# Moving the Q and K row transposes from TensorE to VectorE in a segment-recurrent attention kernel

## Chip, cores, metric

One core of one Trainium2 chip. The metric is device time in microseconds (us), median of several executions. The kernel before takes 2215.26 us (2214.29 to 2218.69, 4 runs).

## The reference, cut

```python
# A: 64 segments of 32 tokens, one after the other; B is a gated FFN over all tokens, done before the loop
for s in range(n_seg):                                   # S=2048, seg_len=32, M=8, Dm=640, H=32, Dh=192
    h = concat([mem, x[:, 32*s:32*s+32]], axis=1)        # 40 rows
    q, k, v = (einsum('btd,dhe->bhte', h, W) for W in (Wq, Wk, Wv))
    p = softmax(where(mask, einsum('bhqe,bhke->bhqk', q, k) * scale, -1e9))
    o = einsum('bhte,hed->btd', einsum('bhqk,bhke->bhqe', p, v), Wo)
    mem = o[:, :M]                                       # the next segment needs this
    outs.append(o[:, M:])
return g * concat(outs) + (1 - g) * ffn                  # g = sigmoid(x . gate_w)
```

The recurrence through `mem` makes the 64 segments serial. Every segment reads all of Wq, Wk, Wv and Wo, 31 MB; the kernel keeps part of that in SBUF and fetches the rest anew in every segment.

## The kernel before, where the change touches it

After about 292 us of preparation (the FFN, and the part of Q and K that does not depend on `mem`) comes the loop of 64 segments. The 32 heads go in four octets of 8 heads (1536 columns). Weights are cut into 84 pieces of a segment; 60 stay resident in SBUF and 24 are streamed in every segment through a ring of five slots, issued in program order from the SP queue when a slot comes free. A cost table (`COST`) places the 24 streamed pieces evenly over the estimated time of a segment.

Q (and K) of an octet is computed with the 32 tokens as the stationary operand. Four column tiles of TensorE work at once, each on 384 columns, so the result is four strips of rows [32 tokens, 384]. Scores need the transpose of that, so the rows are copied to SBUF, transposed by TensorE, and copied back once more:

```python
def cmode(s, m, o, bank):                                # m: 0 = Q, 1 = K
    for k in range(KT):                                  # KT = 5
        g_, rg_ = piece(s, (m, o, k))
        S_.add("pe", [lambda e, ...: e.matmul(ps[32*j:32*j+32, bank, 0:384], Hb[hb][:, k, 0:L],
            g_[:, 384*j:384*(j+1)], ..., tile_position=(0, 32*j)) for j in range(4)], ...)
def rows_evac(bank):                                     # ScalarE: ps -> rows_sb (one buffer)
    ...
def row_transp(s, m, o):                                 # three 128x128 TensorE transposes
    bank = misc_bank(); pv = psb(bank)
    S_.add("pe", [lambda e, c=c: e.transpose(pv[:, c*128:(c+1)*128], rows_sb[:, c*128:(c+1)*128], ident)
                  for c in range(3)], ...)
    # Q: one VectorE copy to Qs; K: three ScalarE copies to Ks     [cut]
PROG = [("q",0), ("k",0), ("tq",0), ("v",0), ("tk",0),   # order of the stages of one segment
        ("q",1), ("k",1), ("sc",0), ("tq",1), ("v",1), ("tk",1),
        ("q",2), ("k",2), ("pt",0), ("sc",1), ("tq",2), ("pv",0), ("v",2), ("tk",2), ...]   # [cut]
```

`sc` is scores and the whole softmax, `pt` the transpose of the probabilities with its evacuation, `pv` P times V, `wo` the output projection. Every fourth segment also computes a second V for the leftover tokens.

## Time and profile before

| | before |
|---|---|
| time | 2215.26 us |
| mean of 62 segments (between memory evacuations) | 29.55 us; every fourth 30.92 |
| of that: Q/K/V phase, Wo phase | 19.45, 10.10 us |
| DMA in the loop | 9.26 MB per segment, 313 GB/s, share 0.93 |

The two phases are my cut at the first Wo matmul of each segment, with the windows view over each part.

The page of the kernel before: busy times of the whole execution, and of its costliest groups those that the change touches (engine, operation, output<-input, count, busy us, mean ns of one, then idle time ahead of them and who ended it). PE is TensorE's matmuls, PEld its weight loads, DVE is VectorE, ACT is ScalarE, POOL is GpSimd.

```profile
PE 1912.3 (86%) x41834; PEld 1231.3 (55%) x41862; DVE 943.6 (42%) x3184; ACT 799.7 (36%) x2248; POOL 273.6 (12%) x1210
...
L871 PE MATMUL ps<-arena 128*32 128x384 bf16 x10240 | 488.1, 330 | 69.6 <-DMA arena<-in_A_Wk_dram 23.6
...
L883 PE MATMUL ps<-arena 128*128 128x128 bf16 x1536 | 175.9, 223 | 32.0 <-ACT arena L877 31.9
...
L894 ACT ACTIVATE arena<-ps 64x128 bf16<-64x128 bf16 x512 | 136.8, 267 | 6.3
L887 DVE COPY arena<-ps 128x384 bf16<-128x384 bf16 x256 | 89.4, 349 | 102.0 <-PE ps L883 102.0
```

L871 are the Q and K matmuls, L883 the row transposes (1536 of them, 176 us of busy PE), L894 and L887 two of the copies behind them. The 176 us are tempting, but PE is not simply the limit, as the windows view over the loop shows (us, then busy time of each engine in the order above, granted clock, DMA share, GB/s; the granted clock is the share of its full clock that TensorE was given):

```profile
353.48:2185.74 1832.26, 1585.06 (x39121) 1065.21 (x39121) 835.57 (x2957) 701.85 (x2062) 258.51 (x1146) 0.99 0.93 313
```

The DMA engines are occupied for 93% of the loop while PE is for 87%. The list of waits of PE inside the loop (353 to 2186 us; who waited for whom, us in total, times, longest):

```profile
PE ps L991 <- DVE arena L977: 38.2, 109, 0.4
PE ps L1020 <- DVE arena L1007: 36.4, 105, 0.5
PE ps L905 <- DMA arena<-in_A_Wv_dram: 27.7, 40, 1.8
PE ps L1020 <- DMA arena<-in_A_Wo_dram: 23.2, 43, 2.0
PE ps L905 <- ACT arena L877: 21.4, 40, 0.8
PE ps L871 <- DMA arena<-in_A_Wk_dram: 20.6, 40, 1.2
...
PE ps L871 <- DMA arena<-in_A_Wq_dram: 13.0, 26, 1.1
PE ps L883 <- ACT arena L877: 12.0, 41, 0.3
```

84 us are waits for weight pieces, 83 us for VectorE, 56 us for ScalarE. The timeline of PE (start, duration, then as above) shows what one group of row transposes costs in place:

```profile
1041.29 0.34 PE L883 MATMUL ps<-arena 128*128 128x128 bf16 x3
1041.56 1.81 PE L905 MATMUL ps<-arena 128*32 128x384 bf16 x40
1043.30 0.34 PE L883 MATMUL ps<-arena 128*128 128x128 bf16 x3
1043.57 1.88 PE L871 MATMUL ps<-arena 128*32 128x384 bf16 x40
```

From the start of a group to the next start is 0.27 us, and there are eight groups per segment.

### The profile page before, as it was taken

What the parts mean: (1) busy time and instruction counts of PE and PEld (TensorE: products, weight loads), DVE (VectorE), ACT (ScalarE), POOL (GpSimd) and SP (SyncE); (2) the same over time, 40 slices, a digit from 0 to 9 for tenths busy, and PEclk for the clock granted to TensorE, in tenths of its full rate; (3) what the DMA queues carried; (4) which work ended last, traced back from release to release, by engine and by line L of the source; (5) the groups of instructions that cost most, each with busy time, mean ns of one, the idle gap of its engine ahead of it and who ended that gap; (6) DMA issues with size and microseconds to landing.
All of it is one profiled execution on the core that took longest, in us unless ns stands there. A gap on an engine that the chain in (4) does not pass through costs nothing.

```text
span 2220.5 us, 94985 instructions
## 1 busy us (share of the span) xinstructions
PE 1912.3 (86%) x41834; PEld 1231.3 (55%) x41862; DVE 943.6 (42%) x3184; ACT 799.7 (36%) x2248; POOL 273.6 (12%) x1210
## 2 busy tenths in 40 slices
PE   7999958888888888888888888888888888888887
PEld 3544425555555555555565655555555655555655
DVE  2222223444444444444444444444444544444444
ACT  2222223334333333343333333333333334333333
POOL 0000001111111111111111111111111111111111
PEclk9999989999999999999999999999999999999999
DMA  9203579999999999999999999999999999999998
GB/s 370 88 13 112 150 236 331 322 303 316 301 318 307 324 303 311 305 316 312 319 320 311 316 300 320 306 313 310 320 302 321 309 322 311 315 315 316 310 309 278
DMA packets 363257, 642.75 MB, mean 289 GB/s; under 512 B 60498, under 2 KB 231770, under 8 KB 362842
## 3 DMA queue, kind: packets, MB, share of 16 engines
q1 hardware_dynamic: 311770, 601.01, 80.2%
q10 hardware_dynamic: 51072, 35.66, 5.4%
q8 instruction: 327, 5.36, 0.9%
q14 instruction: 88, 0.72, 0.1%
HBM read 618.74 MB, written 17.83 MB: 287 GB/s over the span
## 4 chain that ended last, share of the span: by engine, by line
PE 46%; DMA 32%; DVE 14%; ACT 3%; issue 3%; ACTq 2%; SPq 0%; DVEq 0%
PE ps L871 12%; DMA arena<-in_A_Wv_dram 10%; DMA arena<-in_A_Wo_dram 9%; PE ps L1020 9%; DMA arena<-in_A_Wk_dram 8%; PE ps L905 7%; DMA arena<-in_A_Wq_dram 4%; DVE arena L974 4%; PE ps L804 3%; PE ps L883 2%; PE ps L742 2%; PE ps L739 2%; ACTq L819 2%; PE ps L757 2%; DVE ps L954 2%
## 5 line engine op out<-in xcount | busy, mean ns | idle before, releaser
L871 PE MATMUL ps<-arena 128*32 128x384 bf16 x10240 | 488.1, 330 | 69.6 <-DMA arena<-in_A_Wk_dram 23.6
L1020 PE MATMUL ps<-arena 128*128 128x40 bf16 x15360 | 457.9, 180 | 64.8 <-DVE arena L1007 38.1
L1020 PEld LDWEIGHTS ps<-arena 128*128 128x128 bf16 x15360 | 428.9, 96 | 88.8 <-DVE arena L1007 49.5
L871 PEld LDWEIGHTS ps<-arena 128*32 128x32 bf16 x10240 | 247.1, 97 | 254.6 <-DMA arena<-in_A_Wk_dram 63.2
L905 PE MATMUL ps<-arena 128*32 128x384 bf16 x6400 | 324.4, 331 | 53.3 <-DMA arena<-in_A_Wv_dram 30.2
L877 ACT ACTIVATE arena<-ps 128x384 bf16<-128x384 f32 x512 | 249.8, 488 | 181.0 <-PE ps L871 105.1
L974 DVE TENSOR_TENSOR arena<-ps,arena 128x320 bf16<-128x320 bf16 x256 | 125.8, 491 | 387.0 <-PE ps L972 387.0
L835 POOL COPY arena<-arena 128x96 bf16<-128x96 bf16 x256 | 67.4, 263 | 1665.0 <-PE ps L937 1138.3
L956 ACT ACTIVATE ps<-ps 104x160 f32<-104x160 f32 x256 | 71.9, 281 | 494.5 <-DVE ps L954 494.5
L905 PEld LDWEIGHTS ps<-arena 128*32 128x32 bf16 x6400 | 144.6, 96 | 175.5 <-DMA arena<-in_A_Wv_dram 59.2
L883 PE MATMUL ps<-arena 128*128 128x128 bf16 x1536 | 175.9, 223 | 32.0 <-ACT arena L877 31.9
L1001 ACT ACTIVATE arena<-ps 128x320 bf16<-128x320 f32 x256 | 112.3, 439 | 215.4 <-PE ps L993 213.8
L991 PE MATMUL ps<-arena 128*128 128x160 bf16 (+1 forms) x768 | 130.5, 260 | 57.1 <-DVE arena L977 39.6
L916 ACT ACTIVATE arena<-ps 128x384 bf16<-128x384 f32 x256 | 125.6, 491 | 139.0 <-PE ps L905 138.7
L839 POOL COPY arena<-arena 64x32 bf16<-64x32 bf16 (+1 forms) x768 | 165.4, 215 | 47.3
L883 PEld LDWEIGHTS ps<-arena 128*128 128x128 bf16 x1536 | 88.1, 98 | 135.7 <-ACT arena L877 91.1
L952 DVE TENSOR_REDUCE arena<-ps 104x4 f32<-104x160 f32 x256 | 80.9, 316 | 149.3 <-PE ps L937 149.3
L894 ACT ACTIVATE arena<-ps 64x128 bf16<-64x128 bf16 x512 | 136.8, 267 | 6.3
L887 DVE COPY arena<-ps 128x384 bf16<-128x384 bf16 x256 | 89.4, 349 | 102.0 <-PE ps L883 102.0
L993 PE MATMUL ps<-arena 128*128 128x64 bf16 (+1 forms) x768 | 124.5, 202 | 4.0 <-ACT arena L877 4.0
L958 DVE TENSOR_REDUCE arena<-ps 104x4 f32<-104x160 f32 x256 | 83.1, 325 | 99.8 <-ACT ps L956 99.8
L991 PEld LDWEIGHTS ps<-arena 128*128 128x128 bf16 x768 | 72.3, 97 | 91.2 <-DVE arena L977 90.7
(81 smaller groups left out, 1886.3 us busy)
## 6 DMA issues: line engine op xcount, KB each, us to landing
arena<-in_A_Wo_dram SPq DMA_DIRECT2D x591, 320.0 KB, 4.7
arena<-in_A_Wv_dram SPq DMA_DIRECT2D x398, 384.0 KB, 5.2
arena<-in_A_Wk_dram SPq DMA_DIRECT2D x340, 384.0 KB, 5.3
arena<-in_A_Wq_dram SPq DMA_DIRECT2D x276, 384.0 KB, 5.0
left_qk_scratch<-arena ACTq DMA_DIRECT2D x16, 768.0 KB, 8.7
arena<-left_qk_scratch ACTq DMA_DIRECT2D x64, 192.0 KB, 4.6
arena<-in_A_x_dram SPq DMA_DIRECT2D x4, 640.0 KB, 15.0
ffn_b_scratch<-arena ACTq DMA_DIRECT2D x16, 160.0 KB, 1.8
```

What stands on the lines that cost most here:

```text
L839: S_.add("pool", lambda e, a=a, b=b, lo=lo, hi=hi, sa=sa: e.tensor_copy(out=Ks[lo:hi, a:b, L:R], in_=stg[lo:hi, o, 1, sa:sa + b - a]), rea ...
L871: S_.add("pe", [lambda e, j=j, k=k, g_=g_: e.matmul(ps[32 * j:32 * j + 32, bank, 0:384], Hb[hb][:, k, 0:L], g_[:, 384 * j:384 * (j + 1)], ...
L877: S_.add("act", lambda e: e.activation(out=rows_sb, in_=ps[:, bank, 0:384], func=ACTF.Copy), reads=[r_ps[bank]], writes=[r_rows], name="ro ...
L883: S_.add("pe", [lambda e, c=c: e.transpose(pv[:, c * 128:(c + 1) * 128], rows_sb[:, c * 128:(c + 1) * 128], ident) for c in range(3)], rea ...
L894: S_.add("act", lambda e, a=a, lo=lo: e.activation(out=Ks[lo:lo + 64, a:a + 4, 0:L], in_=src[lo:lo + 64, 1], func=ACTF.Copy), reads=[r_ps[ ...
L905: return [lambda e, j=j: e.matmul(ps[32 * j:32 * j + 32, bk, 0:384], lhs, g_[:, 384 * j:384 * (j + 1)], start=(k == 0), stop=(k == KT - 1) ...
L916: S_.add("act", lambda e: e.activation(out=v_sb[o % NVB], in_=ps[:, bank, 0:384], func=ACTF.Copy), reads=[r_ps[bank]], writes=[r_v[o % NVB ...
L974: S_.add("dve", lambda e: e.tensor_tensor(out=PTm, in0=apx(pv[:, 512:616], [[64, 2], [0, 4], [1, R]]), in1=apx(mbd, [[0, 2], [1, 4], [0, R]]),
L991: return [lambda e: e.matmul(full, v[:, e0:e0 + 128], PTm[:, ia:ib], start=True, stop=False, skip_group_check=True), lambda e: e.matmul(pa ...
L993: lambda e: e.matmul(part, vl[:, e0:e0 + 128], PTl[:, ia:ib], start=False, stop=True, skip_group_check=True)]
L1001: S_.add("act", lambda e: e.activation(out=apx(u[:, 0, 0, :], [[2 * R, 2], [3 * R, 4], [1, R]]), in_=ps[:, A, 0:2 * W].rearrange("p (c t r ...
L1020: fns.append(lambda e, g_=g_, i=i, c=c, n=n, tl=tl, cc=cc, u=u: e.matmul(ps[:, OB, n * R:(n + 1) * R], g_[:, i, n * 128:(n + 1) * 128], u[ ...
```

## The change

Intent: VectorE can transpose 32x32 blocks. If column tile j takes not 384 neighbouring columns but the 32-column strip j of each of the 12 chunks of 128, then each 32x32 block of the rows already stands in the right partition group, and a block transpose in place is the whole transpose. TensorE loses the transposes, PSUM a bank use, ScalarE the K copies. The stages are reordered so that a transpose on VectorE runs under other matmuls, and the softmax is divided (max and subtract in `sc`, the rest in `ex`). With the order and `COST` the choice of the 24 streamed pieces changes too: 6 Q, 4 K, 5 V, 9 Wo in place of 4, 5, 6, 9, the same bytes.

```diff
-    rows_sb = bview(wsB_off["rows"], 768)
+    rows_sb = [bview(wsB_off["rows"] + b * 768, 768) for b in range(2)]
-    PROG = [("q", 0), ("k", 0), ("tq", 0), ("v", 0), ("tk", 0), ...
+    PROG = [("q", 0), ("tq", 0), ("k", 0), ("tk", 0), ("v", 0),
+            ("q", 1), ("sc", 0), ("tq", 1), ("k", 1), ("ex", 0), ("tk", 1), ("v", 1),
+            ("q", 2), ("pt", 0), ("sc", 1), ("tq", 2), ("k", 2), ("ex", 1), ("tk", 2), ("pv", 0), ("v", 2), ...
-    COST = dict(q=0.17, k=0.17, v=0.2, sc=0.6, pt=0.2, pv=0.5, wo=0.27, tq=0.2, tk=0.2)
+    COST = dict(q=0.17, k=0.17, v=0.2, sc=0.5, pt=0.2, pv=0.5, wo=0.26, tq=0.0, tk=0.0, ex=0.0)
@@ cmode
-                ps[32*j:32*j+32, bank, 0:384], Hb[hb][:, k, 0:L], g_[:, 384 * j:384 * (j + 1)],
+            gv = g_.rearrange("p (c j i) -> p j c i", c=12, j=4)
+                ps[32*j:32*j+32, bank, 0:384].rearrange("p (c i) -> p c i", i=32), Hb[hb][:, k, 0:L], gv[:, j],
@@ row_transp
-        three e.transpose on "pe" into PSUM, then one "dve" copy (Q) or three "act" copies (K)
+        S_.add("dve", ... e.transpose(out=Qs[:, :, 0:L], in_=rows_sb[0].rearrange("p (c r) -> p c r", r=L)) ...)   # Q
+        S_.add("dve", ... e.transpose(out=apx(Ks[:, 0, :], [[2*R, 4], [R, 2], [1, L]]),
+                                      in_=apx(rows_sb[1], [[96, 4], [64, 2], [1, L]])) ...)                        # K
+        S_.add("dve", ... e.transpose(out=Ks[lo:lo+64, a:a+4, 0:L], in_=src[lo:lo+64, :, 1]) ...)                  # K, twice
```

## The prediction

> **What bounds the kernel now.** The granted-clock row is at full speed in the main loop, so clock is not the subject. After about 292 us of preparation come 64 recurrent segments; between the memory evacuations that end them (a list of that instruction's starts) a segment takes 29.55 us on average, 28.4 to 29.6 for ordinary ones and 30.9 for every fourth, which also computes the second V. The windows view gives, for one segment: PE busy 25.6 us, DVE 13.5, ACT 11.3, DMA share 0.94 at 314 GB/s, 9.26 MB. Two limits lie close together: PE with its short waits, and DMA. 314/0.94 = 334 GB/s, so 9.26 MB cannot take less than about 27.6 us (estimate; the best segments reached 330 GB/s and 27.0 to 27.9 us). In the list of waits PE loses 84 us in the loop to weight DMAs and about 140 us to short DVE and ACT hand-overs.
>
> **Removed.** Eight groups of three TensorE transposes per segment. From the timeline, 20 projection matmuls plus one group start 1.2 us apart, against 0.85 us for half of an uninterrupted 40: 0.3 to 0.4 us per group with the change of tile shape, about 2.8 us of PE per segment. Also PE's wait for the row copy before it (L883, L905, L993 on ACT: 37 us in all), three ACT evacuations per octet (0.38 + 2 x 0.27 us, 234 us in all) and the 0.35 us Q evacuation on DVE.
>
> **Added.** Four DVE block transposes per octet: 128x384, 128x256, twice 64x128. The DVE casts here run at one element per cycle (128x128: 0.29 us, 384: 0.56, 512: 0.69), so I estimate 0.56 + 0.43 + 2 x 0.29 = 1.57 us per octet, net +1.2 us, about +5 us of DVE per segment (13.5 to 18.5) and DVE busy 944 to about 1250 us. The Trainium skill ("VectorE: DVE Perf Modes", The three transpose paths) has 311 ns for 128x128, which agrees with the cast's slope; no run here shows it yet.
>
> **Unchanged, I expect.** The Q and K matmuls now read 64-byte runs at a step of 256 bytes. The skill ("SBUF — State Buffer", cachelines) puts the penalty at runs shorter than two hits per 16-byte line, so no slowdown: 40 of them still in about 1.75 us. The streamed pieces stay 24 per segment, 8.85 MB, in another mix (6 Q, 4 K, 5 V, 9 Wo).
>
> **On the critical path.** PE gains 2.8 + 0.5 us per segment, but not all counts. In octets 2 and 3 DVE now has about 5 us of serial work (P evacuation, max, sub, Tq, sum, reciprocal, p, Tk, uT) against 3.7 us of PE; adding durations along that chain by hand, scores wait for Tk about 0.8 us in three octets, and PV for the P evacuation about 1 us once. That returns 2 us or so. And DMA's 27.6 us stops what is left: DMA waits grow. I expect 28.3 to 28.5 us per segment, a gain of 1.1 to 1.2 us x 64 = about 74 us.
>
> **Time: 2140 us**, 2070 to 2195 (8 in 10). Faster by over 2%: 0.74; within 2%: 0.22; slower: 0.04.
>
> **What would show it.** Right: no PE transposes of rows, PE busy down about 170 us, DVE near 1250, ACT near 565; transposes of 0.56/0.43/0.29 us; PE's score matmuls wait on the K transposes and PE's weight waits on DMA grow; DMA near 325 GB/s in the loop. Every-fourth segments shorten as well, by a us or more.
>
> **What would make it wrong.** DVE transposes at two cycles per element (DVE 23 us per segment, no gain); or faster ones, so only DMA binds (2080 us). Strided moving reads that slow the Q/K matmuls: at double time +7 us per segment, a loss. DMA sustaining 345 GB/s, which gives 2080.

## The result

| | before | after |
|---|---|---|
| time, median (range, 4 runs) | 2215.26 (2214.29 to 2218.69) | 2165.85 (2155.84 to 2168.30) |
| ratio | | 0.9768, 95% interval 0.9737 to 0.9798 |
| mean segment; every fourth | 29.55; 30.92 us | 28.68; 29.13 us |
| Q/K/V phase, Wo phase | 19.45, 10.10 us | 18.20, 10.47 us |
| mean granted clock | 0.986 | 0.978 |

A ratio here is the mean time of one kernel's runs over that of the other's of the same rounds, so it is not quite the ratio of the medians. The gain is 49 us, 0.77 us per segment. The result passes the comparison with the reference.

The same lines of the page after:

```profile
PE 1836.7 (85%) x40326; PEld 1154.9 (53%) x40326; DVE 1231.5 (57%) x3952; ACT 618.8 (29%) x1480; POOL 274.1 (13%) x1210
...
L872 PE MATMUL ps<-arena 128*32 128x384 bf16 x10240 | 566.8, 331 | 119.9 <-DMA arena<-in_A_Wq_dram 77.6
...
L882 DVE STREAM_TRANSPOSE arena<-arena 128x384 bf16<-128x384 bf16 x256 | 146.0, 570 | 102.3 <-ACT arena L876 102.3
...
L889 DVE STREAM_TRANSPOSE arena<-arena 64x128 bf16<-64x128 bf16 x512 | 145.5, 284 | 8.1
...
L885 DVE STREAM_TRANSPOSE arena<-arena 128x256 bf16<-128x256 bf16 x256 | 111.4, 435 | 16.1 <-ACT arena L876 16.1
```

The row transposes are gone from PE and stand on VectorE at 570, 435 and twice 284 ns, as estimated (0.56, 0.43, 0.29). But PE's busy time fell by 76 us, not by the 176 of the transposes: busy of the Q and K group grew from 488 to 567. And the idle time ahead of the Q and K matmuls grew from 70 to 120 us. The loop in the windows view, and PE's waits in it (353 to 2140 us):

```profile
353.06:2130.94 1777.88, 1511.81 (x37633) 991.04 (x37633) 1114.60 (x3701) 527.03 (x1318) 258.99 (x1146) 0.98 0.96 323
```

```profile
PE ps L872 <- DMA arena<-in_A_Wq_dram: 75.5, 125, 1.9
PE ps L992 <- DVE arena L978: 36.9, 98, 0.7
PE ps L1021 <- DVE arena L1008: 34.5, 100, 0.5
PE ps L899 <- DMA arena<-in_A_Wv_dram: 31.3, 49, 1.8
PE ps L1021 <- DMA arena<-in_A_Wo_dram: 29.9, 60, 3.0
...
PE ps L872 <- DMA arena<-in_A_Wk_dram: 10.9, 15, 1.5
...
PE ps L931 <- DVE arena L889: 3.3, 19, 0.4
```

The sum of the waits for weights rose from 84 to 153 us, those for ScalarE fell from 56 to 19, those for VectorE stayed (83 to 81). DMA share went from 0.93 to 0.96. Scores waiting for the K transposes (L931 on L889) are 3 us in the whole loop. So the first reading is theory D: the time that PE saved became time in which it waits for streamed weights. The rival, theory V: the longer serial chain on VectorE took it back. The list of waits speaks for D, but DMA waits can hide VectorE waits behind them, so it does not decide.

The Wo phase, whose matmuls were not changed, became 0.37 us longer; the whole gain lies in the Q/K/V phase (1.25 us). A part of the 0.37 us is the clock: in the clock records of the two traces the Wo phases of these 62 segments ran at half clock for 14 us before and for 41 us after. At half speed at most half of the 27 us more is lost, 0.2 us per segment (estimate).

### The profile page after: what moved, and what is told of

It is laid out like the page before. It is cut to its first block, busy times and chain, and to the rows that moved or that the text cites. A ratio compares the mean times of both kernels' runs of the same rounds, so it can differ in the third digit from the quotient of the medians.

```text
span 2166.5 us, 92005 instructions
## 1 busy us (share of the span) xinstructions
PE 1836.7 (85%) x40326; PEld 1154.9 (53%) x40326; DVE 1231.5 (57%) x3952; ACT 618.8 (29%) x1480; POOL 274.1 (13%) x1210
## 4 chain that ended last, share of the span: by engine, by line
DMA 48%; PE 37%; DVE 9%; ACTq 3%; issue 2%; ACT 2%; SPq 0%; POOL 0%; DVEq 0%; POOLq 0%
DMA arena<-in_A_Wq_dram 19%; DMA arena<-in_A_Wo_dram 13%; DMA arena<-in_A_Wv_dram 10%; PE ps L872 9%; PE ps L1021 7%; PE ps L899 5%; DMA arena<-in_A_Wk_dram 4%; PE ps L804 3%; PE ps L742 2%; ACTq L819 2%; PE ps L739 2%; PE ps L757 2%; PE ps L992 2%; DVE arena L975 2%; DVE arena L1008 1%
## 5 line engine op out<-in xcount | busy, mean ns | idle before, releaser
L872 PE MATMUL ps<-arena 128*32 128x384 bf16 x10240 | 566.8, 331 | 119.9 <-DMA arena<-in_A_Wq_dram 77.6
L1021 PE MATMUL ps<-arena 128*128 128x40 bf16 x15360 | 472.1, 181 | 71.7 <-DVE arena L1008 35.9
L1021 PEld LDWEIGHTS ps<-arena 128*128 128x128 bf16 x15360 | 434.9, 97 | 116.8 <-DVE arena L1008 48.0
L899 PE MATMUL ps<-arena 128*32 128x384 bf16 x6400 | 333.1, 331 | 37.0 <-DMA arena<-in_A_Wv_dram 32.2
L882 DVE STREAM_TRANSPOSE arena<-arena 128x384 bf16<-128x384 bf16 x256 | 146.0, 570 | 102.3 <-ACT arena L876 102.3
L889 DVE STREAM_TRANSPOSE arena<-arena 64x128 bf16<-64x128 bf16 x512 | 145.5, 284 | 8.1
L885 DVE STREAM_TRANSPOSE arena<-arena 128x256 bf16<-128x256 bf16 x256 | 111.4, 435 | 16.1 <-ACT arena L876 16.1
L992 PEld LDWEIGHTS ps<-arena 128*128 128x128 bf16 x768 | 73.9, 99 | 85.5 <-DVE arena L978 60.3
L1006 DVE CAST arena<-ps 64x160 bf16<-64x160 f32 x256 | 80.4, 314 | 52.5 <-PE ps L994 48.4
```

Of the source, the lines that this page charges most:

```text
L872: S_.add("pe", [lambda e, j=j, k=k, gv=gv: e.matmul(ps[32 * j:32 * j + 32, bank, 0:384].rearrange("p (c i) -> p c i", i=32), Hb[hb][:, k, ...
L882: S_.add("dve", lambda e: e.transpose(out=Qs[:, :, 0:L], in_=rows_sb[0].rearrange("p (c r) -> p c r", r=L)), reads=[r_rows[0]], writes=[r_ ...
L885: S_.add("dve", lambda e: e.transpose(out=apx(Ks[:, 0, :], [[2 * R, 4], [R, 2], [1, L]]), in_=apx(rows_sb[1], [[96, 4], [64, 2], [1, L]])) ...
L889: S_.add("dve", lambda e, a=a, lo=lo: e.transpose(out=Ks[lo:lo + 64, a:a + 4, 0:L], in_=src[lo:lo + 64, :, 1]), reads=[r_rows[1]], writes= ...
L899: return [lambda e, j=j: e.matmul(ps[32 * j:32 * j + 32, bk, 0:384], lhs, g_[:, 384 * j:384 * (j + 1)], start=(k == 0), stop=(k == KT - 1) ...
L992: return [lambda e: e.matmul(full, v[:, e0:e0 + 128], PTm[:, ia:ib], start=True, stop=False, skip_group_check=True), lambda e: e.matmul(pa ...
```

## The experiments

Twelve kernels were run. Times are medians of 4 runs (e12: 5); ratios are to the kernel before in the same rounds.

| run | time | ratio |
|---|---|---|
| e1 after, half the streamed bytes | 2016.00 | 0.910 |
| e2 before, half the streamed bytes | 2100.20 | 0.948 |
| e3 block transposes, old stage order | 2220.28 | 1.003 |
| e4 after, contiguous strips | 2169.56 | 0.979 |
| e5 after, half the bytes, cut transposes | 1948.65 | 0.879 |
| e6 after, cut transposes | 2168.98 | 0.978 |
| e7 after, 17 Q/K/V + 6 Wo pieces streamed | 2236.29 | 1.009 |
| e8 TensorE transposes, new order | 2296.09 | 1.036 |
| e9 after, 12 + 12 pieces | 2275.08 | 1.026 |
| e10 after, 4 slots, 12 + 11 pieces | 2348.84 | 1.060 |
| e11 after, the pieces of before | 2188.45 | 0.988 |
| e12 after, 23 pieces, one rows buffer | 2172.96 | 0.981 |

### e1 and e2: take the weight traffic away from both kernels

```diff
 def issue_ring(seg, upto):
-    e.dma_start(piece_view(key, ring_off[slot]), piece_src(key))
+    e.dma_start(*half(key, slot))        # first half of the columns (Wo: first of its two chunks); the rest is stale
```

> The changed kernel, every streamed weight piece of the recurrent loop fetched only in its first half (wrong result on purpose; matmuls, buffers and waits as before). Theory D (weight DMA takes up the TensorE time that was freed): DMA waits of PE nearly vanish, the kernel drops by 2.5 us or more per segment, to 1990 us or less (25.5 us per segment plus 320 us), and the gain over the kernel before, both with half the bytes, is 130 us or more instead of 49. Theory V (the serial VectorE chain took it back): hardly faster than the changed kernel, 2100 us or more, PE waiting for the block transposes and the P evacuation.

> The kernel before, with the same half fetches. Theory D: it loses only its own 1.4 us of DMA waits per segment, to about 2125 us (85 to 95 us less). Theory V: the same, and the changed kernel with half the bytes is within 50 us of it.

Measured: 2016 and 2100 us; both results are wrong. The windows view over the loop of e1, then of e2:

```profile
346.12:1981.23 1635.11, 1446.19 (x37633) 1007.09 (x37633) 1114.80 (x3701) 525.70 (x1318) 258.53 (x1146) 0.99 0.63 183
```

```profile
349.56:2067.03 1717.47, 1537.15 (x39121) 1062.57 (x39121) 835.85 (x2957) 701.57 (x2062) 260.41 (x1146) 1.00 0.59 174
```

With DMA out of the way (share 0.63 and 0.59, under 1 us of DMA waits in the loop) the change is worth 84 us, against 49 with all the bytes. That lies between the two theories' numbers (130 or more for D, 50 or less for V): both missed, each has a part. e2 alone became 115 us faster than the kernel before, where 85 to 95 had been expected from its 84 us of listed waits, so that list understates what the weights cost. To see where the rest stays I added up, from the timeline, the time from each PE group's start to the next start, less the idle time that the timeline lists; e5 (below) is in the same table. Per segment, in us:

| | e2 before | e1 after | e5 after, cut transposes |
|---|---|---|---|
| row transposes | 2.52 | - | - |
| Q, K and V matmuls | 11.61 | 12.06 | 11.91 |
| mask matmuls ahead of scores | 0.33 | 0.62 | 0.38 |
| all of PE's own time | 25.06 | 23.41 | 22.94 |
| listed idle | 2.64 | 2.96 | 2.34 |

Of the 2.52 us removed, 0.87 come back inside other groups. About half of that goes away again when the transposes on VectorE are shortened (e5), so it is waits for VectorE that are too short, or too much overlapped, for the list of waits; some of it is the granted clock, 0.99 in e1 and 1.00 in e2 and e5. 0.64 us of waits for ScalarE's row copies also went (in e2's listed idle), and 0.95 us of VectorE waits came in their place.

### e5 and e6: cut the new VectorE work to half, without and with the weight traffic

```diff
+    nq, nt_ = (12, 4) if s == 0 else (1, 1)     # full in the first segment only
-    e.transpose(out=Qs[:, :, 0:L], in_=...)     # and the K ones likewise with nt_
+    e.transpose(out=Qs[:, 0:nq, 0:L], in_=...[:, 0:nq])
```

> Half the streamed bytes as in e1, and after the first segment every block transpose cut to a small part (one 32-column block each, two for the first K one; wrong result on purpose), all instructions and waits kept. Between e1 and e2 PE's own time fell by only 1.6 us per segment although the removed row transposes took 2.5: Q/K matmuls (+0.8) and the mask matmuls (+0.4) hold short waits that the trace does not list as idle. Theory V (those and the listed waits on VectorE come from the VectorE chain with the transposes in it): about 1.3 us per segment or more comes back, 1940 us or less against 2016. Rival S (the loss is TensorE's own: more tile shape switches or the strided strips): 2000 us or more.

> The changed kernel with all its bytes and the same cut transposes (wrong result on purpose). Theory D (with full bytes DMA holds the pace, so a shorter VectorE chain is worth little): 2140 to 2165 us, PE's DMA waits up by about what the VectorE waits go down. Theory V (VectorE is the pace also here): the same drop as from e1 to e5, to 2090 us or less.

The cut transposes are shorter, not free: in e5's trace they take 204, 237 and twice 184 ns, 0.81 us per octet in place of 1.57.

Measured: 1948.65 with half the bytes (67 us less than e1; I had set 1940 as the line for V, so V's mechanism is there at slightly less than the size named) and 2168.98 with all of them, which is the changed kernel's own time (4 us above D's range, far from V's 2090). Halving the time of the block transposes is worth 67 us when weights are plentiful and nothing when they are not. In the loop of e6 the list of waits has the same DMA lines as the changed kernel:

```profile
PE ps L872 <- DMA arena<-in_A_Wq_dram: 74.5, 134, 2.2
...
PE ps L872 <- DMA arena<-in_A_Wk_dram: 23.2, 37, 1.4
```

The Wk line rose from 10.9 to 23.2 us: what VectorE no longer holds back, the weights do. Together, e2 to e5 is 152 us (2.4 us per segment): that much, at least, freeing PE is worth with the weights out of the way, for half of the transposes' time is still there. The whole VectorE chain leaves 84 of it (e1), and the supply of weights leaves 47 even with the short transposes (e6). At full bytes, then, the weight supply decides, and this part of VectorE's work is hidden under it.

### e4: do the strided strips cost PE time?

```diff
-    gv = g_.rearrange("p (c j i) -> p j c i", c=12, j=4)
+    gv = g_.rearrange("p (j c i) -> p j c i", c=12, j=4)   # strips contiguous again
```

> The changed kernel with each column tile reading its 384 columns contiguously, as before (wrong result on purpose). If the strided strips cost nothing, as predicted: same time within 0.5%, 40 projection matmuls in 1.81 us in both. If they cost something: faster by 20 us or more, and fewer microseconds per 20 matmuls.

Measured: 2169.56 us, 0.2% off the changed kernel, one matmul 333 ns against 331, and 40 of them 1.81 us in both. The strips are free. A caution: this kernel pairs Q and K columns wrongly and still passed the comparison with the reference, as did e6. The comparison does not see errors in Q and K here; that the change itself is right rests on the index argument of its section.

### e3 and e8: each half of the change alone

```diff
 # e3: changed kernel, same streamed pieces, but
-    PROG of after
+    PROG of before, with ("ex", i) directly behind each ("sc", i)
 # e8: changed kernel, same streamed pieces, but row_transp of before (TensorE) and contiguous strips
```

> The block transposes and the strided strips, but the octet stages in the order of before (softmax undivided), the same streamed pieces as the changed kernel. Theory D: when DMA sets the pace the order hardly matters: within 1% of the changed kernel, 2150 to 2185 us. Theory V (the reordering is what hides the VectorE chain): clearly slower than the changed kernel, 2200 us or more.

> The new stage order and the split softmax with the TensorE transposes and the contiguous strips of before, streaming the pieces of the changed kernel. Each transpose then follows its own projection at once and must wait for the row copy [...]: eight times 0.6 to 0.8 us per segment on PE, part of it hidden under DMA waits. All theories: slower than the kernel before, 2300 us or more; a time under 2215 would mean that the order alone brings the gain.

Measured: 2220.28 and 2296.09 us. e3 falls as V had it: without the reordering the block transposes gain nothing, although D's reading says that the order should hardly matter. In its list of waits (353 to 2180 us) scores (L935) and mask (L924) now wait for the K transposes, and P times V (L996) waits about twice as long as in the changed kernel (70.9 against 36.9 us):

```profile
PE ps L996 <- DVE arena L982: 70.9, 211, 0.4
PE ps L876 <- DMA arena<-in_A_Wk_dram: 66.1, 139, 2.0
PE ps L876 <- DMA arena<-in_A_Wq_dram: 47.4, 94, 1.7
...
PE ps L924 <- DVE arena L893: 17.7, 36, 0.9
PE ps L935 <- DVE arena L893: 15.1, 28, 0.9
```

One reservation: e3 streams pieces that were placed for the new order, so a part of its loss may be their placement (the reverse mismatch, e11, costs 22 us). e8 came out as a loss of the expected kind (2296 against 2300 or more): TensorE transposes right behind their own matmuls wait 170 us for the row copies (same window).

```profile
PE ps L886 <- ACT arena L880: 170.3, 338, 0.6
```

So neither half alone, with these pieces, is faster than the kernel before. That the order is what makes the transposes on VectorE fit is the likely reading of e3, within that reservation.

### e7, e9, e10, e11: which pieces are streamed

```diff
-    streamed = chosen by COST, evenly in estimated time
+    streamed = FORCED      # e7: 17 Q/K/V + 6 Wo (8.65 MB per segment, 2.2% less), evenly by count in each phase
+                           # e9: 12 + 12 (8.65 MB);  e10: 12 + 11, ring of 4 slots (8.32 MB);  e11: the 24 of the kernel before
```

> The changed kernel, result right, but 17 Q/K/V and 6 Wo pieces streamed per segment (8.65 MB in 23 pieces) in place of 15 and 9 (8.85 MB in 24). By the packet times of the trace (3072 bytes 140 ns, 1280 bytes 62 ns on average) the DMA work per segment falls from 25.8 to 25.1 us. Theory D: 0.4 to 0.8 us less per segment, 2115 to 2140 us. Theory V: within 10 us of the changed kernel.

> The changed kernel, result right, streaming 12 Q/K/V and 12 Wo pieces per segment (8.65 MB in 24), evenly spaced in each phase. e7 moved the mix to Q/K/V and got slower although its bytes were fewer: DMA share 0.95 in its Q/K/V phase, 0.87 in its Wo phase. Theory B (the Q/K/V phase is the one that DMA holds back, so what counts is the bytes per phase against the 5 pieces of look-ahead, not the total): faster than the changed kernel by 15 to 50 us, 2115 to 2150 us, DMA waits of Q/K/V matmuls down. Rival P (placement of single pieces, not phases): no clear direction; slower if the Wo phase now starves, 2170 us or more.

> The changed kernel, result right, with 4 ring slots in place of 5; the freed 3 KB per partition leaves 12 Q/K/V and 11 Wo pieces to stream (8.32 MB, 6% fewer bytes). Theory D in its plain form (packet throughput is the limit): 1.2 to 1.6 us less per segment, 2070 to 2095 us. Rival L (look-ahead is the limit: with four pieces of about 5 us each in flight DMA idles more): DMA share well under 0.95 and no gain, 2150 us or more.

> The changed kernel, result right, but streaming the very pieces that the kernel before streamed (4 Q, 5 K, 6 V, 9 Wo; the same bytes). If the new choice of pieces is part of the gain: slower than the changed kernel by 10 us or more (2177 us or more). If it only follows the order, as the prediction took it: within 10 us, 2156 to 2176.

Measured: 2236, 2275 and 2349 us for the three with fewer bytes, all far slower than the changed kernel. D in its plain form (fewer bytes, less time) missed each time, and so did V in e7 and B in e9; the rivals' lines (P in e9, 2170 us or more; L in e10, 2150 or more) held. In e7 the Q/K/V phase grew to 19.77 us while DMA's share in the Wo phase sank to 0.87; in e9 it is the reverse, Q/K/V 17.80 us (less than the 18.20 of the changed kernel, as theory B had it) but Wo 12.42. The list of waits of e9 (353 to 2180 us) has the Wo matmuls (L1025) at the top and short Q and K lines:

```profile
PE ps L1025 <- DMA arena<-in_A_Wo_dram: 114.3, 217, 2.6
...
PE ps L876 <- DMA arena<-in_A_Wk_dram: 18.1, 24, 1.4
...
PE ps L876 <- DMA arena<-in_A_Wq_dram: 14.5, 24, 1.3
```

But the listed waits account for little of what e9 lost. By the timeline sums its DMA waits are 2.63 us per segment, against 2.43 in the changed kernel; of the 1.55 us by which its segment is longer, 1.17 are PE's own time. The windows view over its loop shows why (third number from the right, the granted clock: 0.93 against 0.98):

```profile
350.48:2224.25 1873.77, 1576.63 (x37633) 1053.19 (x37633) 1113.51 (x3701) 526.79 (x1318) 258.50 (x1146) 0.93 0.91 300
```

PE ran at half clock for 259 us of this loop, against 58 us in the changed kernel's; at half speed up to 100 of the 109 us lost can be that (estimate). In e7 it is the waits themselves: DMA waits of 3.11 us per segment and VectorE waits of 1.72 (2.43 and 1.31 in the changed kernel), with PE's own time unchanged.

My reading is that pieces must arrive in each phase at the rate at which PE uses them there, and that five slots of look-ahead do not carry a surplus of one phase over to the other. It is argued, not shown: e7 and e9 also space the pieces by count and not by estimated time, so the placement of single pieces (rival P) is not ruled out. e10 changes two things at once against the changed kernel, the ring and the mix. Against e9, which streams the same Q/K/V pieces and ran in the same rounds, it has one slot and one Wo piece less: it moves 3.8% fewer bytes and takes 74 us more, with DMA's share down from 0.91 to 0.87 and the Wo waits up from 114 to 165 us in the same window. That points to the look-ahead, though the places of the Wo pieces moved too.

e11, with all else as in the changed kernel, takes 2188.45 us, ratio 0.988 (0.983 to 0.993) against 0.977 (0.974 to 0.980). So about 22 of the 49 us hang on the new choice of pieces, which comes with the new order and `COST`. The prediction and this expectation's second half had called it neutral.

### e12: fewer bytes, evenly placed

```diff
-    wsB["rows"] = al(2 * 768)              # + 40x40 unit matrix and small constants, each in 64 bytes
+    wsB["rows"] = al(768)                  # Q and K rows share one buffer; unit matrix = ident[:, 0:40]; 16-byte packing
```

> The changed kernel, result right, with 1.2 KB per partition won back (one rows buffer for Q and K instead of two, the 40-column unit matrix taken from the identity, small constants packed at 16 bytes), so that one weight piece more stays resident: 23 streamed pieces (14 Q/K/V, 9 Wo; 8.45 MB, 4.4% less), spread evenly over the time of a segment by the kernel's own rule, 5 ring slots as before. Theory D (packets of streamed weights, evenly spread, hold the pace): 0.7 to 1.1 us less per segment, 2095 to 2125 us, although the single rows buffer makes the VectorE and ScalarE hand-over tighter (e6: that chain is not the pace). Rival P (piece placement or look-ahead alone, not bytes): 2155 us or more.

Measured: 2172.96 us, no faster. D's number missed and P's held, but the waits do not bear out P's reason (that bytes do not matter):

```profile
PE ps L984 <- DVE arena L970: 94.0, 138, 1.5
PE ps L1013 <- DVE arena L1000: 42.5, 117, 0.5
PE ps L864 <- DMA arena<-in_A_Wk_dram: 21.9, 44, 1.5
...
PE ps L864 <- DMA arena<-in_A_Wq_dram: 19.0, 31, 2.4
```

By the timeline sums, DMA waits fell from 2.43 to 1.03 us per segment, so one evenly placed piece less does relieve the supply. But VectorE waits grew from 1.31 to 3.12, because the single rows buffer makes ScalarE's row copies wait for the block transposes that still read it (116 us for the Q and 143 us for the last K transpose in all, 2 and 14 us in the changed kernel). The loss sits in every fourth segment, 30.51 us against 29.13; the other three became shorter, 28.10 against 28.54. The second limit lies directly under the first: the experiment moved one and pressed on the other. I found no version faster than the changed kernel. What 23 pieces with two rows buffers would do stays open, and so does whether a sixth slot would help.

## Why the prediction was right, and where not

The time (2140 predicted, 2165.85 measured, range 2070 to 2195) and the direction held; the gain was 49 us where 74 was named.

- Durations on VectorE: right (570, 435, 284 ns; VectorE busy 1231 for 1250). The Trainium skill, "VectorE: DVE Perf Modes", The three transpose paths, has 311 ns for 128x128; the nearest here, 64x128, took 284, and the slope of the four sizes at 128 partitions (last section) gives 304 for that size (estimate).
- Strips: right, shown by e4. The skill's "SBUF — State Buffer" (the note on cachelines) agrees: 64-byte runs carried no penalty.
- "PE gains 2.8 + 0.5 us per segment": too large as a gain. The pieces were there (2.52 of transposes, 0.64 of ScalarE waits, e2), but with DMA made light and VectorE's new work halved only 2.4 us arrived (e2 to e5): 0.4 us came back inside other groups and 0.3 us as listed waits for VectorE. The same step made "PE busy down about 170 us" wrong: it went down 76, because the busy time of the Q and K group rose by 79. Such a matmul is recorded as 331 ns while 40 of them last only 1.81 us together, so the records overlap, and a short wait between two lies under them and counts as busy. The busy time of a removed group is not the busy time that goes.
- "That returns 2 us or so" (scores 0.8 us in three octets, PV 1 us): wrong at full bytes, and in place. Halving the transposes brings 1.05 us when weights are plentiful (e1 against e5), so the whole chain may well return 2 us there, but nothing at full bytes (e6 against the changed kernel). Scores wait 3 us for the K transposes in the whole loop, not 2.4 us per segment, and PV waits no longer for the P evacuation than before (36.9 us against 38.2).
- "DMA's 27.6 us stops what is left: DMA waits grow": right, and the step that decides. Waits for weights rose from 84 to 153 us, the rate to 323 GB/s (predicted near 325). But I derived a floor from total bytes; e7 and e9 show that bytes alone do not set the pace, which pieces are streamed and where counts too. The segment took 28.68 us, not 28.3 to 28.5.
- "Clock is not the subject": not quite. The mean granted clock went from 0.986 to 0.978, and PE's time at half clock in the loop from 27 to 58 us. Up to 15 of the 25 us that are missing from the predicted gain can be that (estimate: half of the 31 us more). The profiled run had the lowest clock of the four (0.978 to 0.984), so this is an upper figure.
- "Another mix" of streamed pieces, listed under unchanged: wrong, worth about 22 us (e11).
- Every fourth segment shorter by a us or more: right (1.8 us). These have 3 us more of PE work for the same streamed bytes, so there the freed PE time counts most.
- ScalarE near 565 us busy: 619. The removed copies' 234 us are a sum of durations; they overlap each other and other work of ScalarE, so that only 181 us of busy time went.
- The number is partly luck. Without the new choice of pieces, which the prediction took for neutral, the gain is about 27 us, 1.2% (e11). And the 3.3 us of gain and the 2 us of return, both too large at full bytes, offset each other.

That supply holds the pace is shown by e1, e2, e5 and e6; that bytes alone do not tell the supply, by e7, e9 and e11. That it is the rate within a phase is argued. Whether the packets' speed or the look-ahead of five slots is the tighter part of it is not settled; e10 against e9 points to the look-ahead.

## What to carry to other kernels

Before freeing an engine, halve the traffic in a wrong-result copy of both kernels and compare there: the difference (here 84 us for 49) tells how much of the gain the transfers will keep. Where streamed weights run at 0.93 share, as here, the order of stages and the choice of what to stream are part of the change (22 of the 49 us, e11). Look at the granted clock before explaining a loss by listed waits (e9). And when a removed group's busy time is the promise, measure start to start in the timeline, not busy.

## What the Trainium skill lacked or had wrong

- "TensorE: Matmul & The Clock Gate", Part 1: its table gives one idle window of about 3.4 us as what brings the half clock. In the changed kernel the clock halves although PE never idled that long: the longest listed wait in the loop is 3.0 us, and below a single wait of 1.09 us for Wo weights (in 1038 to 1039.1) is followed by three us at half clock. With one of 0.52 us for VectorE before it, the listed idle of the last 3.4 us is 1.6 us. The matmuls bear the record out: 80 of Wo take 3.14 us there, 60 took 1.67 us a little earlier at full clock. The same Part tells of another kernel whose frequent short idle stretches make the clock swing, but gives no duration for them. In these lines of the windows view the third number from the right is the granted clock.

```profile
1037.00:1038.00 1.00, 1.00 (x33) 0.91 (x33) 0.19 (x1) 0.00 (x0) 0.41 (x2) 1.00 1.02 325
1038.00:1039.00 1.00, 0.01 (x1) 0.00 (x0) 0.49 (x2) 0.00 (x0) 0.00 (x0) 1.00 1.10 328
...
1040.00:1041.00 1.00, 0.90 (x28) 0.78 (x25) 0.62 (x2) 0.20 (x1) 0.00 (x0) 0.50 0.97 231
1041.00:1042.00 1.00, 1.00 (x36) 1.00 (x34) 0.00 (x0) 0.00 (x0) 0.00 (x0) 0.50 0.77 254
```

  So a wait for weights can cost twice. Which waits bring the half clock is not settled: with half the bytes and no weight waits the loop's clock is 1.00 (e2) or 0.99 (e1), but the mean clock follows neither the waits for Wo weights nor those for all weights (e7: 0.972 with 5 us for Wo and 193 in all; e9: 0.936 with 118 and 163, each over its own loop).
- "VectorE: DVE Perf Modes", The three transpose paths: one size only. Here 204 ns for 128x32, 237 for 128x64 (both e5), 435 for 128x256, 570 for 128x384: 1.04 ns per column over a fixed 0.17 us. On 64 partitions 184 ns for 64x32 (e5) and 284 for 64x128.
- "SBUF — State Buffer", the note on cachelines: it does not say how a matmul's moving operand fares. With 64-byte runs at a step of 256 bytes, four column tiles side by side, it took 331 ns against 333 contiguous (e4).
- "Perfetto Trace Analysis", Identifying the Most-Contended Engine, calls DMA occupancy misleading and names HBM utilization in its place. These runs agree on the first, but neither number tells what another choice of streamed pieces will do: from a share of 0.96 and 323 GB/s, 2.2% fewer bytes in another placement cost 70 us (e7, 0.92 and 305 GB/s) and 109 us (e9, 0.91 and 300 GB/s).
